# First unit of the first MoE as two half units of 128 tokens

## The chip, the cores and the metric

The kernel runs on one core of a Trainium2 chip. It is one program whose instructions stand in one queue per engine: TensorE (PE in the rows, its weight loads PEld), VectorE (DVE), ScalarE (ACT), GpSimd (POOL), and SyncE (SP), which issues the DMAs. The metric is the device time of one execution in microseconds (us); a kernel's time is the median of its runs.

## The reference

Attention with a bias that depends on the relative position, then two MoE layers on all 2304 tokens. Every output has to be close to the 32-bit reference, so the kernel splits operands into two 16-bit parts (high and low) and multiplies high by high, high by low and low by high.

```python
scores = scale * np.matmul(q, k.transpose(0, 1, 3, 2))       # 4 batches, 8 heads, 576 x 576
bias = np.maximum(x @ w1 + b1, 0.0) @ w2                     # x: from the relative position
attn = softmax(scores + bias)
x = np.matmul(attn, v)                                       # -> 2304 tokens x 512
g = x @ w_gate                                               # first MoE: 512 -> 1536 -> 512
x = (silu(g) * (x @ w_val)) @ w_out
h = np.maximum(x @ w_in, 0.0)                                # second MoE: 512 -> 2048 -> 512
out = h * h @ w_out2
```

## The kernel before

**Attention** goes over the queries in tiles: tile 0 has queries 0 to 127 of all batches and heads, then come tiles 1, 2, 3 and a merged one with the last 64 queries. A tile of 128 queries has 32 items, each one batch and one head, batch by batch; I number them from 1, so batch 0 is items 1 to 8, batch 1 items 9 to 16, and item 33 is the first of tile 1. An item is: scores on PE (4 matmuls, L813), bias and minimum on DVE (L822), the exponential on ACT (L827), five transposes on PE (L851, L853), a copy out of PSUM on ACT (L854), and the product with V on PE (L865, `av`). Before the items of a tile, and beside those of the tile ahead, the tile's bias is made (L644 on PE, masks L605 on DVE).

During tile 0 three more things go on. The keys are prepared in eight groups of four heads (`prep_k`): split into parts (L197 on POOL, L191 on DVE), turned by PE in three steps (L706) and copied out by ACT (L708); K group 4 serves items 17 to 20, group 6 items 25 to 28. The **weights stream** (`w_stream`) loads the three matrices of the first MoE, decodes them on DVE (L262, L265, L267), measures them (L324, L361, L328), and splits them (L191, L197, L201, L220). Gate and value come in three column groups, then `w_out` in 12 blocks of rows. The blocks of `w_out` from the eighth on overwrite the raw keys, so they wait for K group 7; the whole of `w_out` must be measured (its sum over partitions goes through PE at L139 and DVE at L141) before its 12 splits (L201 on ACT, L191 on DVE) can begin. The split of one block overwrites what the block after it reads, so the 12 go one after the other.

**The first MoE** works in units of 256 tokens (`moe1`). Unit 0 is batches 0 and 1 of tile 0, unit 1 batches 2 and 3 of it, and so on. When the attention of a unit's tokens is done, `finish_unit` takes their largest norm (a transpose on PE, a reduction on DVE), makes a scale of it on one partition (several DVE instructions on 1x1) and spreads it over the partitions with a matmul (L169), copies it (L908, L909), makes the two 16-bit parts of each 128 tokens in `xh` (L921 on ACT, L922 on DVE; one buffer), and turns them with a DMA into `xT` (L925). Then come 12 blocks of 128 hidden columns, 24 matmuls each on 256 columns (L459), gate and value side by side in one PSUM bank; tanh on ACT (L467), two products on DVE (L468, L470), which free the bank, and the split of the result into `z` (L444 on ACT, L220 on POOL). At the end 72 matmuls on 512 columns multiply `z` by `w_out` (L482), 36 for each half of the unit.

**PSUM** of this stage: `mm` has two banks, for the blocks of the unit, the accumulator of the product with `w_out`, and sums of the weights stream. `ma` is a single bank, for the turns of the keys and queries and for `finish_unit`; its users take turns in the order in which the program was recorded.

**What sets the order.** The instructions are recorded by two generators, attention with the weights stream (`a`) and the MoE units (`m`), each with a position in its own cost units. `m` takes a step when `a` has passed a base plus a table's value (`LEAD`) at `m`'s position. The base is `a`'s position when the first unit of attention is done. Tokens gate steps: `("unit", m)` waits for the attention of unit m, `("w", 3)`, ahead of the product with `w_out`, for the end of the weights stream, `("f", 2)` in that stream, after the second column group, for two blocks of the MoE. What was recorded is then put in order on each engine by the scheduler of the framework; within an engine the queue runs in that order.

## Time and profile before

| | |
|---|---|
| median of 3 runs | 1244.9 us (1240.95 to 1245.37) |
| the profiled execution, its own time | 1241.07 us |
| its span, first to last instruction | 1238.9 us |
| PE busy | 1089.9 us, 88% of the span |
| DVE busy | 778.1 us, 63% |
| ACT busy | 678.0 us, 55% |
| POOL busy | 651.8 us, 53% |
| TensorE clock granted, mean | 0.961 |

Busy shares are means over stages with different limits. Tile 0 of the attention runs to about 215 us, the bias of tile 1 is made from 235 us, tile 1's first item starts at 271 us, and attention ends near 705 us; the rest is the end of the first MoE and the second MoE. Rows of a timeline give start and duration, engine, line, operation, tiles and shape, and in brackets how long the engine had been idle and what ended that. Durations of matmuls overlap, so their cost is read from one start to the next.

### The profile page before, as it was taken

How to read it: one execution, taken by the hardware profiler on the slowest of the kernel's cores; microseconds unless marked ns; L12 is line 12 of the kernel's file. 1: busy time of each engine (PE TensorE's matmuls, PEld its weight loads, DVE VectorE, ACT ScalarE, POOL GpSimd, SP SyncE). 2: the span in 40 equal slices, each digit the busy share in tenths (PEclk: the TensorE clock that was granted, in tenths of full speed). 3: DMA queues.
4: the chain of work that ended last, by engine and by line, in shares of the span. 5: the costliest groups of instructions: out<-in, count | busy, mean ns of one | idle time of the engine just before them, and what ended most of it. 6: DMA issues, size and time to landing. Idle time of an engine off the chain costs nothing.

```text
span 1238.9 us, 27332 instructions
## 1 busy us (share of the span) xinstructions
PE 1089.9 (88%) x10550; PEld 812.1 (66%) x10550; DVE 778.1 (63%) x1864; ACT 678.0 (55%) x1370; POOL 651.8 (53%) x835
## 2 busy tenths in 40 slices
PE   2577899998678889999997999979789999999998
PEld 2466788686467568686774767556348476584787
DVE  5988957887677667656665745895573442624423
ACT  3567767557566566566663543366462643616433
POOL 2433213269768687878784452237791532705423
PEclk9789799999979999999999999989999999999999
DMA  9957543219999998997989995660010010010100
GB/s 222 263 136 206 179 132 87 50 58 198 222 218 204 227 212 165 231 186 162 191 161 257 248 220 142 206 188 1 17 34 19 18 43 27 20 33 17 27 27 17
DMA packets 278078, 163.20 MB, mean 132 GB/s; under 512 B 233276, under 2 KB 246588, under 8 KB 277948
## 3 DMA queue, kind: packets, MB, share of 16 engines
q1 hardware_dynamic: 277948, 161.46, 55.0%
q8 instruction: 82, 1.34, 0.5%
q14 instruction: 48, 0.39, 0.1%
HBM read 92.13 MB, written 19.48 MB: 90 GB/s over the span
## 4 chain that ended last, share of the span: by engine, by line
PE 45%; DMA 14%; POOL 10%; DVE 8%; issue 5%; ACT 4%; SPq 2%; POOLq 0%; ACTq 0%; DVEq 0%
PE mm L1377 12%; PE mm L459 11%; PE mm L1409 10%; DMA pT<-pt 3%; PE mm L482 3%; POOL pt L220 3%; POOL x L1189 2%; PE ma L1409 2%; PE av L875 2%; PE qk L813 2%; DMA w2s<-in_moe_w_out_dram 2%; DMA qT<-qs 2%; DMA scrap<-in_moe_w_in_dram 1%; DMA kp<-kT_d 1%; DMA xT<-xh 1%
## 5 line engine op out<-in xcount | busy, mean ns | idle before, releaser
L459 PE MATMUL mm<-xT,wr 128*128 128x256 f16 x2400 | 288.7, 276 | 14.9 <-DVE th L470 7.3
L459 PEld LDWEIGHTS <-wr 128*128 128x128 f16 x2592 | 251.6, 99 | 53.2 <-issue 19.3
L1189 POOL TENSOR_TENSOR x<-x 128x256 f32<-128x256 f32 (+1 forms) x160 | 142.7, 903 | 178.1 <-ACT x L1386 171.7
L220 POOL TENSOR_TENSOR pt<-s,pt 128x512 f16<-128x512 f32 x224 | 172.1, 791 | 31.5 <-ACT pt L837 26.7
L220 POOL TENSOR_TENSOR z<-th,z 128x256 f16<-128x256 f32 x108 | 79.8, 740 | 129.5 <-ACT z L444 124.7
L482 PE MATMUL mm<-wr,z 128*128 128x512 f16 x612 | 142.3, 379 | 1.6 <-DVE sc L829 1.3
L822 DVE CUSTOM_DVE_ANT_0 s<-qk,room 128x576 f32<-128x576 f32 x144 | 107.7, 748 | 39.9 <-PE qk L813 22.6
L1409 PEld LDWEIGHTS <-wr 128*128 128x128 f16 x1134 | 110.6, 98 | 22.7 <-DVE wr L1189 4.3
L830 ACT ACTIVATE s<-s,sc 128x576 f32<-128x576 f32 x112 | 85.6, 772 | 56.6 <-DVE sc L829 47.1
L1189 DVE TENSOR_TENSOR wr<-x,wr 128x768 f16<-128x768 f32 (+3 forms) x60 | 75.4, 1268 | 64.5 <-ACT wr L1196 63.3
L1377 PE MATMUL mm<-wr,w2r 128*128 128x512 f16 (+1 forms) x480 | 102.2, 364 | 5.0 <-ACT x L1382 5.0
L482 PEld LDWEIGHTS <-z 128*128 128x128 f16 x648 | 60.0, 98 | 66.4 <-issue 2.8
L605 DVE TENSOR_TENSOR scrap<-scrap,room 128x1024 f16<-128x1024 f16 (+1 forms) x108 | 87.3, 822 | 22.4 <-PE ma L644 19.8
L1377 PE MATMUL mm<-wr,room 128*128 128x512 f16 (+1 forms) x480 | 100.1, 358 | 0.0
L621 POOL TENSOR_TENSOR scrap<-scrap 128x256 f32<-128x256 f32 (+1 forms) x90 | 63.2, 702 | 65.9 <-ACT scrap L620 58.2
L875 PE MATMUL av<-vp,pT 128*128 128x65 f16 (+3 forms) x1792 | 70.4, 196 | 28.3 <-DMA pT<-pt 24.3
L875 PEld LDWEIGHTS <-pT 128*128 128x128 f16 (+1 forms) x1792 | 61.7, 102 | 43.2 <-DMA pT<-pt 32.7
L1377 PEld LDWEIGHTS <-w2r 128*128 128x128 f16 x480 | 47.6, 99 | 52.7 <-issue 8.6
L644 PEld LDWEIGHTS <-scrap 128*128 128x128 f16 x1440 | 59.6, 104 | 27.4 <-issue 11.9
L1377 PEld LDWEIGHTS <-room 128*128 128x128 f16 x480 | 46.9, 98 | 45.6
L1428 ACT ACTIVATE ob<-ob,fac 128x256 f32<-128x256 f32 x36 | 17.8, 506 | 105.5 <-DVE ob L1427 105.5
L444 ACT CAST z<-th 128x256 f16<-128x256 f32 x108 | 42.8, 399 | 59.0 <-DVE th L470 57.8
(289 smaller groups left out, 2157.2 us busy)
## 6 DMA issues: line engine op xcount, KB each, us to landing
kp<-kT_d SPq DMA_DIRECT2D x64, 288.0 KB, 3.5
vp<-v_d SPq DMA_DIRECT2D x48, 325.0 KB, 3.5
w2s<-in_moe_w_out_dram SPq DMA_DIRECT2D x16, 512.0 KB, 4.0
wr<-in_moe_w_gate_dram SPq DMA_DIRECT2D x24, 256.0 KB, 5.2
wst<-in_moe_w_out_dram SPq DMA_DIRECT2D x12, 512.0 KB, 4.0
wr<-in_moe_w_val_dram SPq DMA_DIRECT2D x24, 256.0 KB, 4.2
v_d<-vp SPq DMA_DIRECT2D x16, 325.0 KB, 3.1
y_d<-yh SPq DMA_DIRECT2D x18, 256.0 KB, 3.5
```

The lines of the kernel that those rows point to most:

```text
L220: nc.gpsimd.tensor_tensor(out=out_, in0=x, in1=hi, op=ALU.subtract)
L459: nc.tensor.matmul(pg[:, 256 * gi:256 * gi + 256], wr.parts(key, f // 4, cc, wl, P * (f % 4), P), mov(xl, cc), start=k == 0, stop=k == 11)
L482: nc.tensor.matmul(po, zall[:, f, zl, P * t:P * t + P], wr.parts("o", 0, f, wl), start=k == 0, stop=k == 3 * NF1 - 1)
L605: nc.vector.tensor_tensor(out=m[:, :, ni * e:ni * e + ni], in0=block(kb, i0, ni), in1=th, op=ALU.is_gt)
L621: nc.gpsimd.tensor_tensor(out=tmp[r], in0=tmp[r], in1=xb, op=ALU.mult)
L644: nc.tensor.matmul(pv[:, :, :, c:c + 4], m[:, a, :], bd[:, l], start=l == 0, stop=l == 1)
L822: nc.vector.tensor_tensor_reduce(out=s.rearrange("p (a j) -> p a j", a=2), in0=pq[:, :, 0:288], in1=bias[:, n].rearrange("p (a j) -> p a j ...
L830: nc.scalar.activation(s, s, AF.Exp, bias=nm, scale=-1.0)
L875: nc.tensor.matmul(av[r, slot, 0:cn], pT[:, 5 * l + c, r], vs[e][c][:, c0:c0 + cn], start=m == 0, stop=m == 13)
L1189: (nc.gpsimd if how else nc.vector).tensor_tensor(out=out_, in0=a, in1=b, op=op)
L1377: nc.tensor.matmul(ph[:, :n], w2r.parts("w", g // 4, cc, wl, P * (g % 4), P), yt[:, 4 * yl + cc, :], start=m == 0, stop=m == 11)
L1409: nc.tensor.matmul(po, HS[f][:, o:o + P], st["C7"][f][wl][:, b:b + 256], start=f == 0 and k == 0, stop=f == 7 and k == 2)
```

## The change

Unit 0 alone is computed as two half units. `finish_unit` is called after batch 0 and again after batch 1, each time for 128 tokens, and both write their half of one `xT`. `moe1` runs twice, first for the tokens of batch 0, then for those of batch 1, with the same instructions on 128 columns in place of 256. The product with `w_out` has as many instructions as before, 36 for each half, and the weights stream's gate for it stands: the first half's product and all of the second half are recorded after the end of the weights stream. The base is now `a`'s position at the end of batch 0, 11.2 cost units earlier; `LEAD` has 11.2 more at its points from 39 on, so that unit 1 and all units after it are recorded at the same places beside the attention as before.

```diff
-LEAD = [0, 39, 78, 117, 260, 400], [0, 85.669, 132.183, 165.544, 287.094, 406.094]
+LEAD = [0, 20, 39, 78, 117, 260, 400], [0, 48.0, 96.87, 143.383, 176.744, 298.294, 417.294]
+HALVED = (0,)
...
-    def moe1(m):
-
-        yield ("unit", m)
-        xt, sx = xT.pop(m), ux.pop(m)
+    def moe1(m, half=None):
+
+        yield ("unit", m if half != 0 else m - 0.5)
+        n = 256 if half is None else P
+        b0 = P if half else 0
+        xt, sx = xT[m, half], ux[m, half]
...
-                            pg[:, 256 * gi:256 * gi + 256], wr.parts(key, f // 4, cc, wl, P * (f % 4), P),
+                            pg[:, n * gi:n * gi + n], wr.parts(key, f // 4, cc, wl, P * (f % 4), P),
...
-            yield 2.6
+            yield 2.6 * n / 256
...
         yield ("w", 3)
-        for t in range(2):
+        for t in range(2) if half is None else (half,):
...
-    def finish_unit(u, xs_, nrm):
-
-        m1 = scr([P, 1], tag="fm")
-        nc.vector.tensor_reduce(out=m1, in_=nrm, axis=AX, op=ALU.max)
+    def finish_unit(u, xs_, nrm, half=None):
+
+        m1 = nrm
+        if half is None:
+            m1 = scr([P, 1], tag="fm")
+            nc.vector.tensor_reduce(out=m1, in_=nrm, axis=AX, op=ALU.max)
...
-        t = (mw2[0] if more else mw).tile([P, 2, 4, 256], F16, tag="xT", name="xT")
+        t = xT[u, 0] if half else (mw2[0] if more else mw).tile([P, 2, 4, 256], F16, tag="xT", name="xT")
...
-                if i == (3 if merged else 1):
+                u = state["u"]
+                if u in HALVED:
+                    yield ("fin", u)
+                    finish_unit(u, state["xs"], state["nrm"][:, 0:1], b % 2)
+                    done[0] = u - 0.5 if b % 2 == 0 else u
+                    state.update(u=u + b % 2, xs=[], nrm=None)
+                elif i == (3 if merged else 1):
...
-        if done[0] >= 0 and w_done[0] >= 0 and base is None:
+        if done[0] > -1 and w_done[0] >= 0 and base is None:
```

In the changed program the lines stand 1 to 14 further down (L706 is L711, L822 is L827, L921 is L928, L459 is L463, L482 is L487). Counted in the order of PE: before, the first matmul of unit 0 stands after the scores of item 24, 192 of its 288 stand ahead of the last items' products with V, and 96 of them and 41 of the 72 matmuls with `w_out` stand between the last product with V and the first matmul of tile 1's bias. Now there are 576 short ones. The first stands after the scores of item 16, 48 stand ahead of those of item 17, all 288 of the first half ahead of those of item 25, and none between those of items 25 and 32. The 288 of the second half and 66 of the 72 matmuls with `w_out` stand between the end of tile 0 and the first matmul of the bias. Of unit 1, 144 matmuls (six blocks) stood between that bias matmul and the scores of item 33, now 192 (eight blocks). From the scores of item 82 on, PE's order is the same row by row; the other engines' orders rejoin near the same place.

On PE, before, the first turn of K group 4 (the last row here) stands behind item 8's product with V, after the scores of item 9:

```order
L848 MATMUL tr<-qT,ident_h 128x512
L851 MATMUL tr<-ident,s 128x128 x4
L853 MATMUL tr<-ident,s 128x128
L865 MATMUL av<-wr,pT 128x64 x5
L706 LDWEIGHTS room_114
L706 MATMUL ma<-ident_h,room_114 128x128
```

On PE in the changed program the same turn (L711) stands behind the spread of the first half unit's scale in `ma` (the second L170), after the scores of item 16:

```order
L853 MATMUL tr<-qT,ident_h 128x512
L856 MATMUL tr<-ident,s 128x128 x4
L858 MATMUL tr<-ident,s 128x128
L870 MATMUL av<-room_114,pT 128x64 x10
L170 MATMUL mm<-sc,ones_r 128x2
L170 MATMUL ma<-sc,ones_r 128x2
L711 LDWEIGHTS room_114
L711 MATMUL ma<-ident_h,room_114 128x128
```

What moved is the turn: the half unit's two uses of the single bank now come ahead of it, and all three turns of the group stand together behind them.

On ACT, before, the two halves of unit 0's `xh` (L921) stand among the items, with the exponential of a later item behind the second:

```order
L361 ACTIVATE wst,keep_2097<-wr,keep_2091 128x512
L854 COPY pT<-tr 128x640
L827 ACTIVATE s,sc<-s,sc 128x576
L921 ACTIVATE xh<-room_114,ux 128x512
L854 COPY pT<-tr 128x640
L921 ACTIVATE xh<-room_114,ux 128x512
L827 ACTIVATE s,sc<-s,sc 128x576
L708 COPY kva<-ma 128x4x256
```

On ACT in the changed program the first half's `xh` (L928) stands alone, with the turned keys of group 4 (L713) and the first short tanh (L471) behind it; the second half's `xh` comes 53 rows later:

```order
L832 ACTIVATE s,sc<-s,sc 128x576
L362 ACTIVATE wst,keep_1873<-wr,keep_1865 128x512 x2
L928 ACTIVATE xh<-room_114,ux 128x512
L713 COPY kva<-ma 128x4x256 x2
L713 COPY kva<-ma 128x4x64
L362 ACTIVATE wst,keep_1873<-wr,keep_1865 128x512 x2
L471 ACTIVATE th<-mm,ux 128x128
```

What moved is that no second `xh` follows the first, and that work on `w_out` (L362) and the keys stand there instead.

On DVE, before, the measure of `w_out` (L364, then the copy of its sum, L141) stands among the products of unit 0's blocks, all 32 items' scores being past:

```order
L265 SCALAR_TENSOR_TENSOR wr<-wst,wr 128x512
L191 SCALAR_TENSOR_TENSOR wr<-wr,keep_2045 128x512
L470 SCALAR_TENSOR_TENSOR th<-th,mm 128x256
L267 SCALAR_TENSOR_TENSOR wr<-wst,wr 128x512
L468 SCALAR_TENSOR_TENSOR th<-th,mm 128x256
L191 SCALAR_TENSOR_TENSOR wr<-wr,keep_2045 128x512
L470 SCALAR_TENSOR_TENSOR th<-th,mm 128x256
L364 TENSOR_REDUCE sc<-keep_2097 128x1
```

On DVE in the changed program the same measure (L365, L142) stands among the last items (L827, the pair of rows that takes an item's scores), before those of item 32:

```order
L827 ISA s,sc<-qk,room_115 128x576
L827 ISA sc 128x1
L263 TENSOR_SCALAR wr<-wst 128x512
L756 COPY qs<-qs 128x4x64
L266 SCALAR_TENSOR_TENSOR wr<-wst,wr 128x512
L268 SCALAR_TENSOR_TENSOR wr<-wst,wr 128x512
L827 ISA s,sc<-qk,room_115 128x576
L827 ISA sc 128x1
L365 TENSOR_REDUCE sc<-keep_1873 128x1
L900 TENSOR_TENSOR room_114<-av,sc 128x256
L827 ISA s,sc<-qk,room_115 128x576
L827 ISA sc 128x1
```

What moved is the attention against the weights stream: in each stretch from item 17 on, the stream is further ahead of the items than it was.

## Rows read from the trace of the kernel before

**Rows 1.** Stretches of 20 us: busy us (instructions) of PE, PEld, DVE, ACT, POOL; clock, DMA share, GB/s.

```profile
120.00:140.00 20.00, 15.13 (x131) 13.39 (x131) 20.00 (x45) 15.42 (x31) 7.77 (x6) 0.91 0.68 211
140.00:160.00 20.00, 17.34 (x90) 15.11 (x90) 13.34 (x39) 10.75 (x25) 3.17 (x2) 0.59 0.56 169
160.00:180.00 20.00, 18.31 (x192) 16.70 (x192) 11.04 (x25) 16.42 (x31) 3.62 (x3) 0.99 0.28 78
180.00:200.00 20.00, 17.05 (x160) 15.16 (x160) 15.57 (x54) 18.62 (x42) 5.99 (x7) 1.00 0.52 151
300.00:320.00 20.00, 18.52 (x197) 11.33 (x197) 14.21 (x36) 14.99 (x34) 19.57 (x28) 1.00 1.05 221
```

**Rows 2.** Timeline of PE, items 24 and 25 and unit 0's first block.

```profile
160.74 0.65 PE L813 MATMUL qk<-room,qT 128*128 128x288 f16 x4
...
164.77 2.79 PE L459 MATMUL mm<-xT,wr 128*128 128x256 f16 x24
...
172.57 0.65 PE L813 MATMUL qk<-kva,qT 128*128 128x288 f16 x4
```

**Rows 3.** Timeline of ACT, the two halves of unit 0's xh.

```profile
153.51 0.71 ACT L921 ACTIVATE xh<-room,ux 128x512 f16<-128x512 f32 x1
...
160.07 0.72 ACT L921 ACTIVATE xh<-room,ux 128x512 f16<-128x512 f32 x1 [5.12 <-DMA xT<-xh]
```

**Rows 4.** Timeline of PE from tile 0's end to item 33.

```profile
176.43 0.61 PE L706 MATMUL ma<-ident_h,room 128*128 128x128 f16 x8
176.87 0.65 PE L813 MATMUL qk<-kva,qT 128*128 128x288 f16 x4
...
197.20 0.65 PE L813 MATMUL qk<-room,qT 128*128 128x288 f16 x4
...
230.35 5.14 PE L482 MATMUL mm<-wr,z 128*128 128x512 f16 x23
235.33 0.57 PE L644 MATMUL qk<-bd,scrap 128*128 128x64 f16 x14
...
256.67 2.78 PE L459 MATMUL mm<-xT,wr 128*128 128x256 f16 x24
259.29 1.10 PE L644 MATMUL qk<-bd,scrap 128*128 128x64 f16 x32
...
270.64 0.65 PE L813 MATMUL qk<-kp,qT 128*128 128x288 f16 x4
```

**Rows 5.** Timeline of ACT and DVE: what frees one block's bank.

```profile
167.60 0.48 ACT L467 ACTIVATE th<-mm,ux 128x256 f32<-128x256 f32 x1 [0.74 <-PE mm L459]
...
168.11 0.42 DVE L468 SCALAR_TENSOR_TENSOR th<-th,mm 128x256 f32<-128x256 f32 x1 [1.94 <-ACT th L467]
...
168.57 0.42 DVE L470 SCALAR_TENSOR_TENSOR th<-th,mm 128x256 f32<-128x256 f32 x1
```

**Rows 6.** DVE's instructions of 112 to 147 us by form: count, busy us, mean ns.

```profile
L191 DVE SCALAR_TENSOR_TENSOR wr<-wr,keep 128x512 f16<-128x512 f32 x6 | 4.5, 742 | 0.7 <-POOL wr L197 0.6
...
L191 DVE SCALAR_TENSOR_TENSOR room<-wr,room 128x1280 f16<-128x1280 f32 x2 | 3.0, 1476 | 0.0
L267 DVE SCALAR_TENSOR_TENSOR wr<-wst,wr 128x512 int32<-128x512 int32 x4 | 2.6, 674 | 0.0
...
L166 DVE TENSOR_SCALAR sc<-sc 1x1 f32<-1x1 f32 x2 | 0.3, 133 | 0.0
```

**Rows 7.** Timeline of PE, K group 4's first turn and item 17's scores.

```profile
99.79 0.61 PE L706 MATMUL ma<-ident_h,room 128*128 128x128 f16 x8
...
130.64 0.65 PE L813 MATMUL qk<-kva,qT 128*128 128x288 f16 x4
```

**Rows 8.** Timeline of DVE, w_out's sum and its first and last split.

```profile
213.13 0.15 DVE L141 COPY sc<-mm 1x1 f32<-1x1 f32 x1
...
216.62 0.75 DVE L191 SCALAR_TENSOR_TENSOR wr<-wr,keep 128x512 f16<-128x512 f32 x1 [0.59 <-ACT wr L201]
...
237.03 0.74 DVE L191 SCALAR_TENSOR_TENSOR wr<-wr,keep 128x512 f16<-128x512 f32 x1
```

More of the change, by code (lines that the diff above doesn't have):

```diff
@@ L437, in mov @@
             if m < 8:
-                return xt[:, l, cc, :]
+                return xt[:, l, cc, b0:b0 + n]
             pair = xt[:, l, 2 * (cc // 2):2 * (cc // 2) + 2, :].rearrange("p c t -> p (c t)")
@@ L443, in finish @@
             with tc.high_priority():
-                nc.scalar.copy(zall[:, f, 0, :], th)
-                rest_of(zall[:, f, 1, :], th, zall[:, f, 0, :])
+                hi, lo = [zall[:, f, l, b0:b0 + n] for l in range(2)]
+                nc.scalar.copy(hi, th)
+                rest_of(lo, th, hi)
         last = None
@@ L464, in moe1 @@
                     finish(f - 1, last)
-            last = mw.tile([P, 256], F32, tag="th", name="th", bufs=3)
+            last = mw.tile([P, 256], F32, tag="th", name="th", bufs=3)[:, 0:n]
             with tc.high_priority():
-                nc.scalar.activation(last, pg[:, 0:256], AF.Tanh, scale=cg)
+                nc.scalar.activation(last, pg[:, 0:n], AF.Tanh, scale=cg)
                 nc.vector.scalar_tensor_tensor(
-                    out=last, in0=last, scalar=1.0, in1=pg[:, 0:256], op0=ALU.add, op1=ALU.mult)
+                    out=last, in0=last, scalar=1.0, in1=pg[:, 0:n], op0=ALU.add, op1=ALU.mult)
                 nc.vector.scalar_tensor_tensor(
-                    out=last, in0=last, scalar=CZ, in1=pg[:, 256:512], op0=ALU.mult, op1=ALU.mult)
+                    out=last, in0=last, scalar=CZ, in1=pg[:, n:2 * n], op0=ALU.mult, op1=ALU.mult)
             f_done[0] += 1
-            yield 2.6
+            yield 2.6 * n / 256
         finish(NF1 - 1, last)
-        gv_done[0] = m
+        if half != 0:
+            gv_done[0] = m
         yield ("w", 3)
-        for t in range(2):
+        for t in range(2) if half is None else (half,):
             po = mx()
@@ L909, in finish_unit @@
         nc.vector.tensor_copy(sx[:, 1:2], pb[:, 0:1])
-        ux[u] = sx
+        ux[u, half] = sx
         w = 256 if u == 8 else 512
         more = u >= 2 and u % 3 == 2
-        t = (mw2[0] if more else mw).tile([P, 2, 4, 256], F16, tag="xT", name="xT")
+        t = xT[u, 0] if half else (mw2[0] if more else mw).tile([P, 2, 4, 256], F16, tag="xT", name="xT")
         tv = t.rearrange("p l (c d) t -> p l c (d t)", d=512 // w)
-        for i, xx in enumerate(xs_):
+        for i, xx in enumerate(xs_, half or 0):
             k = i * w // 512
@@ L927, in finish_unit @@
                 in_=xh.rearrange("p l e -> p (l e)"))
-        xT[u] = t
+        xT[u, half] = t
     done, w_done, gv_done, f_done, av_done = [-1], [-1], [-1], [0], [0]
@@ L1284, in m_all @@
         for m in range(9):
-            yield from moe1(m)
+            for h in (0, 1) if m in HALVED else (None,):
+                yield from moe1(m, h)
     sa, sm = a_all(), named(m_all(), "m")
```

## The prediction, made before the changed kernel had run

> **What bounds the kernel now.** I first cut the trace into stretches of 20 us [rows 1]. No engine bounds the end of tile 0's attention for long: DVE is busy throughout 120 to 140 us (decoding and splitting weights between the items), 140 to 160 us has every engine partly idle and a granted clock of 0.59 (much of it at the lower level, 1.2 GHz), and from 160 us PE leads with 18.31 and 17.05 of 20 us. In tile 1 POOL (19.57 of 20) and the DMA engines (share 1.05) are full, so there the attention no longer waits for the MoE. What the change can win or lose must therefore show in when item 33, the first of tile 1, starts, now at 270.64 us [rows 4]. Everything behind it follows its predecessors, and from item 82 on PE's order is the same. So the forecast is the shift of item 33, less what tile 1 gives back.
>
> Next I looked for waits around unit 0 in the timelines. Item 25's scores come 11.8 us after item 24's [rows 2], where the seven gaps from item 25 to item 32 take 172.57 to 197.20, 24.6 us, 3.5 us each [rows 2, 4]. In that gap ACT waits 5.12 us for the single `xh` buffer to be read by the first transposing DMA [rows 3], with item exponentials queued behind it. Last, after tile 0 PE does unit 0's remaining blocks and the product with `w_out`, and the bias comes behind them at 235.33 us [rows 4]; that product is held by the 12 splits of `w_out`, which end at 237.8 us, 24.6 us after its sum at 213.13 [rows 8].
>
> **The arithmetic.** PE: 24 matmuls on 256 columns take 2.62 us from start to start, 109 ns each [rows 4], so the unit costs 288 x 109 = 31.4 us. A turn, 128 columns with weights of its own, takes 0.44 us for 8, 55 ns [rows 4]; 576 x 55 = 31.7 us. The doubled weight loads hide, and PE pays nothing. DVE and ACT get 24 instructions more each, POOL 12. A product on 128 columns is not in the trace; it lies between a 1x1 instruction, 0.13 us [rows 6], and the 256-column one, 0.42 us [rows 5]. Two against one then cost between -0.16 and +0.42 us; I take 0.28 us for one, the middle, so +0.14, and 24 x 0.14 = 3.4 us of DVE spread over 100 us in which it has gaps. On the path I count it at nothing while items hide it; uncovered it is 3.4 us (bounds -3.8 to 10). The second `finish_unit` is some ten tiny DVE instructions at 0.13, 1.3 us, and no extra DMA: two transposes as before, now a batch apart.
>
> The Trainium skill bears on these extra instructions, page Perfetto Trace Analysis, section Optimizing Scalar/DVE Operations: each carries a fixed access cost, about 125 ns for DVE on PSUM, and larger operations pay if the engine is saturated. That speaks against the change; by it the 24 products would be 3.0 us (an estimate), beside the 3.4 above, and no row yet has a 128-column one.
>
> **Item 17 moves back.** The new order puts both uses of the `ma` bank by the first half's `finish_unit` ahead of K group 4's turns, which item 17 needs. The first turn ran at 99.79 us, item 17's scores at 130.64 [rows 7]. In DVE's new queue eight more decoding steps (0.67), four splits of weights (0.74), one of keys (1.48), the half's own low part (about 0.74) and four short products (0.28) stand between items 16 and 17 [rows 6]: 5.4 + 3.0 + 1.5 + 0.7 + 1.1 = 11.7 us on an engine that is full just then [rows 1]. Item 17: 130.6 + 11.7 = 142.3. The time isn't lost: the weights stream is ahead by it.
>
> **Items 17 to 25.** All 240 remaining matmuls of the first half stand here, 13.1 us. The gaps of items 25 to 32 held two blocks, 48 x 109 ns = 5.2 us, so a gap without MoE is (24.6 - 5.2)/7 = 2.8 us. Eight of them and the matmuls: 22.2 + 13.1 = 35.3 us if PE is the limit, 8 x 3.5 = 28 if half the matmuls hide. The second half's `finish_unit` again stands ahead of K group 6's turns; of today's long gap, 11.8 - 2.8 - 5.1 = 3.9 us would recur without the wait for `xh`. I take 38, nearer to the first, since PE is already at 86 to 92% there. Item 25: 142 + 38 = 180 (170 to 186), now 172.6.
>
> **The sum of `w_out`.** With its last decoding waiting for K group 7, the sum now comes after item 31. Six gaps of 2.8 are 16.8, and two loads that have to land add about 2: 180 + 19 = 199 (189 to 207), now 213.1. This is the gain of the change, 14 us.
>
> **The bias of tile 1.** Today it starts 22.2 us after that sum (235.33 - 213.13). In the new order the 288 matmuls of the second half (15.8 us) and 66 of the product stand in between; 23 of those take 230.35 to 235.33, 217 ns each [rows 4], so 14.3 us. By PE alone, with the last items and the first split (216.62 + 0.75 is 4.2 us after the sum [rows 8]), about 5 + 15.8 + 14.3 = 35 us. By the splits, the first half's 36 products end no sooner than 24.6 us after the sum; then come 30 more (6.5 us) and some 130 short matmuls (7.1 us): 38 us. I take 40, for both are met only if nothing slips. Bias at 199 + 40 = 239, 4 us later than now: the gain is spent, since the product and the whole second half had to wait for the same sum.
>
> **To item 33.** Now 270.64 - 235.33 = 35.3 us, with 31 products (6.7 us) and six blocks of unit 1 (15.7). Afterwards 6 products (1.3) and eight blocks (20.9), so 35.3 - 5.4 + 5.2 = 35 if idle stays, 31 if it closes. I take 33: item 33 at 272, +1.4 us. Two blocks of unit 1 are then already done, and tile 1, full on POOL, may return up to 1.5 us. The sum is about zero: 1241 us for an execution like the profiled one (1241.07, span 1238.9), and 1245 us against the median of 1244.9, which lies 3.8 us above it.
>
> **Rivals.** (1) **Faster: the attention hides the first half.** If items 17 to 25 keep today's mixed pace, 28 us and the 3.9 of the finish, item 25 comes at 174 and the sum at 193; with 38 and 33 behind it item 33 is at 264, -6.6 us, about 1237 with tile 1's part. For it: ACT's wait of 5.12 us goes, and DVE has gaps of 9 of 20 us after 160 [rows 1]. Against it: PE is the fullest engine there.
>
> (2) **Slower: the banks in the burst.** With 256 columns a block keeps PE for 2.62 us, and its bank is free 0.48 + 0.42 + 0.42 and small gaps, 1.4 us, after its last matmul [rows 5]; with two banks that hides. A short block lasts 1.3 us. While the product holds one of the two `mm` banks, each block waits for the bank of the one before it; if tanh and products take nearly as long as now, or find a split ahead of them (0.74), the wait is 1.4 + 0.7 - 1.3 = 0.8 us a block, 12 x 0.8 = 10 us in the burst, where nothing else can fill it: 1255. It decides from the point where freeing a bank takes longer than the 1.3 us of other matmuls put beside it. The order puts five or six products there, 1.1 to 1.3 us, and a short chain would be about 0.34 + 2 x 0.28 = 0.9.
>
> (3) **Slower: the clock.** From 140 to 160 us PE was granted 0.59, after 20 us in which it was busy 15.13 [rows 1]. With item 17 moved back, PE does less between 128 and 142 us. If the first half's 240 matmuls run at 1.2 GHz, they cost 13.1 us more, two thirds of it on the path since PE leads: +8, 1253. The skill's page TensorE: Matmul & The Clock Gate, section What's actually happening, has the array throttled by default and activity lifting that; by this rule the dense first half would soon raise the clock, which speaks for a smaller price.
>
> That the change does not do what it says is ruled out for the first half by the order (its blocks stand beside items 17 to 24); that the second half gains nothing is in the sum.
>
> **How the numbers follow.** Forecast, no change: 0.48. Rival 1: 0.27. Rival 2: 0.13. Rival 3: 0.12. One measurement of this kernel can tell about 0.5%, 6 us, from no change. Rival 1 lies at that edge and takes most of faster, with a part of the forecast's lower tail; so faster 0.26, same 0.49, slower 0.25. The predicted time is the likeliest case's, 1245. Its own terms (item 25 from 170 to 186, the bias 35 to 42 behind the sum, 31 to 35 to item 33) reach some 8 us to either side when a few of them err together; with the rivals at 1237, 1253 and 1255, leaving out their far tails, the range is 1235 to 1256.
>
> **What would show it.** In the new trace: item 17's scores near 142 us, item 25's near 180, `w_out`'s sum near 199 and thus before item 32, no wait of ACT for `xh` in tile 0, the first bias matmul some 40 us behind the sum, item 33 near 272, and the shift there kept to the end. Item 33 before 265 would be rival 1; gaps before the short matmuls of the burst that DVE ends are rival 2; a granted clock near 0.5 from 142 to 165 us is rival 3. The forecast is wrong in kind if the shift at item 33 isn't the shift at the end.

## The result: 1.1% slower

The changed kernel takes 1259.6 us (median of 6 runs, 1256.6 to 1265.2) against 1245.2 us (6 runs, 1241.0 to 1251.0); the ratio is 1.0111, 95% interval 1.0079 to 1.0144. Four further runs of it in a later series gave 1.0137 (1.0088 to 1.0185). The forecast was no change, 1245 us in a range up to 1256: wrong in kind, and the time lies outside the range.

The profiled execution took 1264.80 us (span 1262.7), 5 us above the median; the profiled one of the kernel before lay 4 us below its own. So of the 23.7 us between the two traces some 14 stand for the kernels.

The stretches of the changed kernel that answer to [rows 1], and the one behind them:

```profile
120.00:140.00 20.00, 13.06 (x107) 11.39 (x107) 18.88 (x52) 9.94 (x21) 8.97 (x7) 0.78 0.54 152
140.00:160.00 20.00, 16.64 (x221) 15.57 (x219) 15.55 (x42) 19.09 (x45) 5.91 (x7) 0.97 0.63 201
160.00:180.00 20.00, 19.13 (x240) 18.11 (x239) 14.91 (x52) 13.98 (x32) 8.68 (x11) 1.00 0.30 77
180.00:200.00 20.00, 14.92 (x170) 13.30 (x168) 15.47 (x39) 17.04 (x38) 4.41 (x5) 0.98 0.51 175
200.00:220.00 20.00, 20.00 (x130) 17.50 (x130) 9.74 (x36) 11.11 (x22) 0.00 (x0) 0.67 0.23 47
```

PE is fuller from 160 to 180 us, as meant, but emptier from 180 to 200 (14.92 against 17.05 us), and then full at a granted clock of 0.67, much of it at 1.2 GHz. The marks on PE's timeline that answer to [rows 2, 4, 7] (first use of `ma` by the first half's `finish_unit`, its second use, first turn of K group 4, item 17, item 25, item 32, first bias matmul, item 33):

```profile
106.36 0.27 PE L132 MATMUL ma<-ident,sc 128*1 128x128 f32 x1
...
130.40 0.36 PE L170 MATMUL ma<-sc,ones_r 1*128 1x2 f32 x2
131.99 1.01 PE L711 MATMUL ma<-ident_h,room 128*128 128x128 f16 x8 [1.23 <-DVE ux L916]
...
144.08 0.65 PE L818 MATMUL qk<-kva,qT 128*128 128x288 f16 x4
...
185.32 0.65 PE L818 MATMUL qk<-kva,qT 128*128 128x288 f16 x4
...
210.76 1.17 PE L818 MATMUL qk<-room,qT 128*128 128x288 f16 x4
...
252.79 0.60 PE L649 MATMUL qk<-bd,scrap 128*128 128x64 f16 x15
...
285.73 0.65 PE L818 MATMUL qk<-kp,qT 128*128 128x288 f16 x4
```

And DVE's that answer to [rows 8], `w_out`'s sum and its first and last split:

```profile
208.17 0.14 DVE L142 COPY sc<-mm 1x1 f32<-1x1 f32 x1
...
214.93 0.75 DVE L192 SCALAR_TENSOR_TENSOR wr<-wr,keep 128x512 f16<-128x512 f32 x1 [0.82 <-ACT wr L202]
...
232.42 0.75 DVE L192 SCALAR_TENSOR_TENSOR wr<-wr,keep 128x512 f16<-128x512 f32 x1 [0.27 <-ACT wr L202]
```

The sum comes 5.0 us earlier than before, not 14; item 33 15.1 us later, not 1.4.

### The profile page after: what moved, and what is told of

It reads as the page before. It is cut to its first block, busy times and chain, and to the rows that moved or that the text cites. A ratio compares the mean times of both kernels' runs of the same rounds, so it can differ in the third digit from the quotient of the medians.

```text
span 1262.7 us, 28025 instructions
## 1 busy us (share of the span) xinstructions
PE 1105.3 (88%) x10841; PEld 824.6 (65%) x10841; DVE 780.5 (62%) x1899; ACT 683.9 (54%) x1394; POOL 658.5 (52%) x847
## 4 chain that ended last, share of the span: by engine, by line
PE 44%; DMA 19%; DVE 12%; POOL 11%; issue 6%; ACT 5%; SPq 1%; POOLq 0%; ACTq 0%; DVEq 0%
PE mm L1391 12%; PE mm L1423 10%; PE mm L463 8%; PE mm L487 5%; DMA pT<-pt 5%; POOL pt L221 3%; DMA qT<-qs 3%; POOL x L1202 2%; PE ma L1423 2%; PE qk L818 2%; DMA wr<-in_v_dram 2%; PE av L880 2%; DMA wr<-in_k_dram 2%; POOL z L221 1%; DVE s L827 1%
## 5 line engine op out<-in xcount | busy, mean ns | idle before, releaser
L463 PE MATMUL mm<-xT,wr 128*128 128x256 f16 (+1 forms) x2688 | 295.3, 265 | 18.4 <-DVE th L474 7.4
L463 PEld LDWEIGHTS <-wr 128*128 128x128 f16 x2880 | 260.8, 100 | 62.3 <-issue 24.6
L221 POOL TENSOR_TENSOR z<-th,z 128x256 f16<-128x256 f32 (+1 forms) x120 | 86.1, 720 | 165.0 <-ACT z L448 159.1
L487 PE MATMUL mm<-wr,z 128*128 128x512 f16 x612 | 146.7, 383 | 0.7 <-DVE th L474 0.4
L827 DVE CUSTOM_DVE_ANT_0 s<-qk,room 128x576 f32<-128x576 f32 x144 | 108.0, 750 | 50.3 <-PE qk L818 36.3
L1423 PEld LDWEIGHTS <-wr 128*128 128x128 f16 x1134 | 110.7, 98 | 20.5 <-DVE wr L1202 3.0
L487 PEld LDWEIGHTS <-z 128*128 128x128 f16 x648 | 60.6, 99 | 65.2 <-issue 4.9
L610 DVE TENSOR_TENSOR scrap<-scrap,room 128x1024 f16<-128x1024 f16 (+1 forms) x108 | 88.9, 838 | 18.7 <-PE ma L649 13.8
L448 ACT CAST z<-th 128x256 f16<-128x256 f32 (+1 forms) x120 | 44.9, 377 | 61.0 <-DVE th L474 60.6
```

The lines of the kernel that those rows point to most:

```text
L221: nc.gpsimd.tensor_tensor(out=out_, in0=x, in1=hi, op=ALU.subtract)
L463: nc.tensor.matmul(pg[:, n * gi:n * gi + n], wr.parts(key, f // 4, cc, wl, P * (f % 4), P), mov(xl, cc), start=k == 0, stop=k == 11)
L487: nc.tensor.matmul(po, zall[:, f, zl, P * t:P * t + P], wr.parts("o", 0, f, wl), start=k == 0, stop=k == 3 * NF1 - 1)
L610: nc.vector.tensor_tensor(out=m[:, :, ni * e:ni * e + ni], in0=block(kb, i0, ni), in1=th, op=ALU.is_gt)
L827: nc.vector.tensor_tensor_reduce(out=s.rearrange("p (a j) -> p a j", a=2), in0=pq[:, :, 0:288], in1=bias[:, n].rearrange("p (a j) -> p a j ...
L1423: nc.tensor.matmul(po, HS[f][:, o:o + P], st["C7"][f][wl][:, b:b + 256], start=f == 0 and k == 0, stop=f == 7 and k == 2)
```

## Experiments, first part: where is the loss?

Three theories stood at first. A: the first half's `finish_unit` holds `ma` (106.4 to 131.7 us), item 17 is late for it, and that lives on. B: the second half has to wait for `w_out`'s sum and makes a burst behind tile 0. C: short blocks cost time by themselves. D was formed on the first four runs: what counts is how much MoE work PE still has between items 32 and 33.

**e1_bank.** Only the first half's two turns move to the `mm` banks:

```diff
-        r = expo(pmax(m1, ma), half=True)
-        pb = spread(r, (2.0 ** 49, 2.0 ** -50), ma)
+        bank = mx if half == 0 else ma
+        r = expo(pmax(m1, bank), half=True)
+        pb = spread(r, (2.0 ** 49, 2.0 ** -50), bank)
```

> The changed kernel with one edit: the first half unit's finish_unit takes its two PSUM turns from the mm banks and not from the single ma bank, so K group 4's turns no longer stand behind it. Theory A (the hold of ma, 106.4 to 131.7 us in the changed kernel, delays item 17 by 13.4 us and that delay lives on to the end): item 17's scores return to 130 to 133 us, item 33's come at 272 to 276, time 1246 to 1250. Theory B (the first half has to share PE and DVE with the items, and the second half waits for w_out's sum anyway): item 17 returns to 130 to 133 too, but item 25 is at 180 or later and item 33 stays at 282 to 287, time 1256 to 1262.

Measured: 1268.5 us, ratio 1.0174 (1.0122 to 1.0226). Its timeline of PE, item 17, the second half's two uses of `ma`, item 25:

```profile
128.67 0.65 PE L818 MATMUL qk<-kva,qT 128*128 128x288 f16 x4
...
140.25 0.42 PE L132 MATMUL ma<-ident,sc 128*1 128x128 f32 x1
...
179.71 0.58 PE L170 MATMUL ma<-sc,ones_r 1*128 1x2 f32 x2
...
190.09 0.65 PE L818 MATMUL qk<-kva,qT 128*128 128x288 f16 x4
```

Item 17 is on time, but the second half now holds `ma` for 39 us and item 25 comes 5 us later still. Items 32 (210.2) and 33 (285.6) stand where they stood, as theory B had it; the time lies above the forecasts of both. Theory A is not refuted by this, since the hold moved; but the gain at item 17 was worth nothing.

**e3_short.** The halves stay, the early start goes: both `finish_unit` calls at the end of batch 1, base and table as before.

```diff
-                    finish_unit(u, state["xs"], state["nrm"][:, 0:1], b % 2)
-                    done[0] = u - 0.5 if b % 2 == 0 else u
+                    if b % 2 == 0:
+                        state["pf"] = (state["xs"], state["nrm"][:, 0:1])
+                    else:
+                        finish_unit(u, *state["pf"], 0)
+                        finish_unit(u, state["xs"], state["nrm"][:, 0:1], 1)
+                        done[0] = u
```

> The changed kernel with both half units finished together at the end of batch 1, and with base and table of the kernel before: the short blocks and their gates without the early start. Theory A (hold of ma): item 17 near 131 and item 33 within 3 us of the kernel before (271 to 274), time 1244 to 1248. Theory B (the second half, gated by w_out's sum, leaves a burst behind tile 0 and two more blocks of unit 1 ahead of item 33): sum to item 33 still takes some 75 us, item 33 at 284 to 290, time 1256 to 1262. Theory C (short blocks cost time by themselves, through banks and DVE): as B, with idle time of PE ahead of short blocks that DVE ends.

Measured: 1270.3 us, 1.0190 (1.0151 to 1.0230). Items 17 (129.7), 25 (171.2) and 32 (198.6) are where they were in the kernel before, and item 33 is at 287.7, 17 us late. All but 1.4 us of that loss arises behind item 32. With item 17 on time the loss is larger than the changed kernel's, so theory A can't be the whole explanation.

**e4_gvfirst and e5_bank_gvfirst.** Both products with `w_out` move behind the blocks of both halves; the second has e1's edit too.

```diff
-        yield ("w", 3)
-        for t in range(2) if half is None else (half,):
+        if half == 0:
+            return
+        yield ("w", 3)
+        for t in range(2):
+            iu = ux[m, None if half is None else t][:, 5:6]
```

> The changed kernel with both products with w_out behind the blocks of both halves, so that the second half's blocks are no longer gated by w_out's sum and can stand among items 25 to 32. Theory A: item 17 stays at 144, item 33 at 283 to 286, time 1257 to 1261. Theory B: no stretch at 1.2 GHz between items 28 and 32 (199 to 213 us in the changed kernel), sum to bias under 38 us instead of 45, item 33 at 275 to 279, time 1249 to 1254.

> Both edits, mm banks for the first finish_unit and products behind both halves. If the two losses add (A and B each in part): item 17 at 130 to 133, item 33 at 264 to 270, time 1238 to 1244, ahead of both kernels. If A alone holds: 1246 to 1250. If PE's work to item 33 sets the time whatever the order: item 33 at 274 to 280, time 1248 to 1254.

Measured: 1259.5 us, 1.0100 (1.0061 to 1.0140), and 1269.1 us, 1.0184 (1.0143 to 1.0224). In e4 the stretch at 1.2 GHz behind item 28 is mostly gone and the bias starts at 243.5, but item 32 comes at 217.2; item 33 at 281.4 (between the two theories) won 4 us, the time nothing. e5 missed by far: item 25 at 197.5, item 33 at 289.7.

**e6_short_gvfirst** is e3 with e4's edit: short blocks, and nothing else of the change.

> Only the short blocks: both half units are finished together at the end of batch 1, base and table are those of the kernel before, and both products with w_out stand behind the blocks of both halves, as in the kernel before. The order of PE has 10 of unit 0's 12 blocks and none of the products ahead of the bias, and 3 blocks fewer of unit 1 ahead of item 33 than before. Theory C (short blocks cost time by themselves): time 1254 to 1262, with idle time of PE that DVE or ACT ends ahead of short blocks. Theory D (what counts is how much MoE work PE still has between items 32 and 33: that stretch was work left plus 21 to 24 us in the kernel before, the changed one and three of the four kernels run so far): 10.65 blocks of 2.62 us, products 15.6 us and 22, so item 33 at 199 + 65 = 264 us, and since 3 blocks (7.9 us) are left for later, time 1240 to 1248.

Measured: 1250.9 us, 1.0035 (1.0010 to 1.0061); item 33 at 269.5, bias at 226.2. Theory C is out as the explanation: short blocks cost at most 0.6%. (The time lies between the forecasts of C and D.) And it differs from e3 in nothing but the place of the first half's product, and so in the second half's blocks no longer waiting for the weights stream; together this is worth 19 us. Its products, on PE's timeline, stand beside the bias:

```profile
238.81 5.56 PE L490 MATMUL mm<-wr,z 128*128 128x512 f16 x25 [0.39 <-DVE th L474]
...
245.14 5.13 PE L490 MATMUL mm<-wr,z 128*128 128x512 f16 x23
...
251.04 5.13 PE L490 MATMUL mm<-wr,z 128*128 128x512 f16 x23
```

**e7_bank2, e8_bank2_gvfirst, e9_before_bank**: both halves' turns on the `mm` banks; the same with e4's edit; and the kernel before with unit 0's turns there.

> The changed kernel with both half units' finish_unit on the mm banks (the run before had the first one only, and the delay moved from item 17 to item 25). Theory A in its new form (each finish_unit that holds ma delays the next K group's turns by 10 to 20 us, the delay lives on): item 17 near 130, item 25 at 165 to 175, item 32 at 194 to 200, time 1246 to 1251. Theory D: item 32 at 194 to 200 with 3.5 blocks of unit 0 done, work left 8.5 + 7 blocks and the products, 40.6 + 15.6 + 22 = 78 us, item 33 at 272 to 278, time 1248 to 1254. If only the gate of the second half counts, as in the run with the late finish: 1264 to 1272.

> Both finish_units on the mm banks and both products behind the blocks of both halves. Theory D: item 32 at 194 to 200 with 3.5 blocks done, 10.5 blocks, products and 22, 27.5 + 15.6 + 22 = 65 us, item 33 at 260 to 265, four blocks of unit 1 (10.5 us) left for later, time 1238 to 1248. Theory A alone: as the run with both finish_units on mm, 1246 to 1251. Theory C: above 1254.

> The kernel before with unit 0's finish_unit on the mm banks, no halves. Its hold of ma, 144.4 to 152.3 us, goes. Theory A: the 11.8 us gap ahead of item 25 shrinks to 4 to 8, item 25 at 164 to 168 instead of 172.6, item 32 at 188 to 194, time 1237 to 1243. Theory D: item 32 at 190 to 195 with 3 blocks done, 14 blocks, products and 22, 74 us, item 33 at 264 to 269, one block left for later, time 1240 to 1246.

Measured: 1275.4 us, 1.0236 (1.0203 to 1.0269); 1266.9 us, 1.0163 (1.0134 to 1.0193); 1243.0 us, 0.9983 (0.9965 to 1.0000). Without the hold of `ma` item 32 comes at 191.9, 192.6 and 188.8, 5 to 8 us before the old 197.2, and item 33 at 294.2, 284.9 and 267.7. e7 is the clearest: 19 us ahead of the changed kernel at item 32, 8.5 us behind it at item 33. Its time ends theory A in its newer form too (each hold of `ma` delays what follows; 1246 to 1251 expected); e8 was as slow as only theory C had it, which e6 rules out. Theory D fits e9 (264 to 269) but put e7 at 272 to 278 and e8 at 260 to 265, so as a rule for item 33 it falls as well.

## Experiments, second part: the scratch tile

What the slow kernels share stands on ACT. The timeline of ACT in the changed kernel: the square of the first half's product (L498), the values' norm (L675), the squares of batches 2 and 3 (L970), and unit 1's `xh` (L928):

```profile
234.39 0.60 ACT L498 ACTIVATE junk<-mm 128x512 bf16<-128x512 f32 x1
...
235.10 1.06 ACT L675 ACTIVATE junk<-kva 128x1024 bf16<-128x1024 f32 x1
...
237.84 0.62 ACT L970 ACTIVATE junk<-room 128x512 bf16<-128x512 f32 x1
...
240.74 0.62 ACT L970 ACTIVATE junk<-room 128x512 bf16<-128x512 f32 x1
...
246.03 0.72 ACT L928 ACTIVATE xh<-room,ux 128x512 f16<-128x512 f32 x1
```

Batch 3's last product with V ended near 219 us, and its square, which opens unit 1's `finish_unit`, comes some 22 us later. In the kernel before, ACT's timeline has the two in the other order:

```profile
214.85 0.63 ACT L963 ACTIVATE junk<-room 128x512 bf16<-128x512 f32 x1 [0.80 <-DVE sc L166]
...
243.34 0.59 ACT L493 ACTIVATE junk<-mm 128x512 bf16<-128x512 f32 x1
```

All these squares want only their sum; the squared values go to one scratch tile, `junk1`. In this program writers of one tile keep the order in which they were recorded. Before, unit 0's product is recorded behind all of tile 0. In the change the first half's product follows its blocks at once when the weights stream ends, at 144.7 of `a`'s cost units, when 22 of the 32 items are recorded to their end. So batch 2's and 3's squares wait for `w_out`'s sum, 12 splits, 36 products and that square. Unit 1's `xh` then frees the room (L928, L929 read it) that tile 1's bias is built in, with the angles from which the masks are made (L597 to L610): in all kernels run the first bias matmul comes 2.6 to 6.9 us after unit 1's first `xh` on DVE, and item 33 33 to 46 us after the bias. This is theory J. It fits the order of ACT in every run: where the product is recorded first (the changed kernel, e1, e3, e7), batch 3's square stands 6.3 to 6.4 us behind the product's and 22 to 33 us behind the last product of its own batch; in the others, within 2.1 us of that.

The end of this chain in the changed kernel, on POOL (the room is cleared as soon as `xh` has been read), DVE (the first two masks) and PE (the work just ahead of the first bias matmul at 252.79):

```profile
247.60 0.10 POOL L597 MEMSET room<- 128x1 f32 x1 [1.17 <-DVE xh L929]
```

```profile
248.04 1.53 DVE L610 TENSOR_TENSOR scrap<-scrap,room 128x1024 f16<-128x1024 f16 x2
```

```profile
250.40 2.55 PE L487 MATMUL mm<-wr,z 128*128 128x512 f16 x11
```

So the masks are ready 3.2 us before the bias, and PE goes from the product to the bias without a pause. From the sum to the bias PE idled only 3.3 of 44.6 us. Two limits thus lie close together here: the chain, which allows no bias before about 249 us, and PE's queue, which has 288 short matmuls and 66 products ahead of it. The second seems to follow from the first: when the chain is cut, PE's order changes with it (below).

**e10_junk, e11_bank2_junk, e12_short_junk**: the square of the product writes to `yh`, which is overwritten next, in the changed kernel, in e7 and in e3.

```diff
-        nc.scalar.activation(junk_tile()[:, 0:512], po, AF.Square, accum_out=ss)
+        yh = mw.tile([P, 2, DM], F16, tag="yh", name="yh", bufs=1)
+        nc.scalar.activation(yh[:, 0, :].bitcast(BF16), po, AF.Square, accum_out=ss)
...
-        yh = mw.tile([P, 2, DM], F16, tag="yh", name="yh", bufs=1)
```

> The changed kernel with one edit: the square of the product with w_out in out_y writes its unused result into yh and no longer into the scratch tile junk1. Theory J: in the changed kernel the squares of batches 2 and 3 of tile 0, which open unit 1's finish_unit, and the norms of the values write junk1 too and are recorded behind that square of the first half's product, so they wait for w_out's sum, 12 splits and 36 products (ACT: the square at 234.4 us, batch 2's and 3's at 237.8 and 240.7, though the last product with V was at 218.9); unit 1's xh frees the room that the bias masks need, so bias and item 33 wait as well. With the edit: squares within 3 us of their batches' last products, unit 1's first xh at 222 to 230, bias at 226 to 234, item 33 at 266 to 274 instead of 285.7, time 1240 to 1250. Theory D (PE's work sets it): item 33 earlier by as much, but the 8 blocks of unit 1 that the order now leaves behind item 33 come back in tile 1, 1256 to 1262. If neither, item 33 at 284 to 287.

> The kernel with both finish_units on the mm banks (1275 us) with the same edit of the scratch tile. Theory J: its items 17 to 32 were 13 to 19 us earlier than in the changed kernel and that was lost behind the same square; now item 32 stays at 190 to 195, bias at 226 to 234, item 33 at 262 to 270, time 1238 to 1248. Theory D: 1256 to 1270.

> The kernel with the late start and the gated second half (1270 us) with the same edit of the scratch tile. Theory J: it was on time at item 32 (198.6 us) and lost 17 us behind the square; now bias at 222 to 230, item 33 at 262 to 270, time 1244 to 1252, near the kernel with the products behind both halves (1251). Theory D: 1262 to 1270.

e10 on ACT (batch 3's square, unit 1's `xh`) and on PE (first bias matmul, item 33):

```profile
221.32 0.61 ACT L970 ACTIVATE junk<-room 128x512 bf16<-128x512 f32 x1
...
227.48 0.71 ACT L928 ACTIVATE xh<-room,ux 128x512 f16<-128x512 f32 x1
```

```profile
231.41 1.17 PE L649 MATMUL qk<-bd,scrap 128*128 128x64 f16 x32
...
269.87 0.65 PE L818 MATMUL qk<-kp,qT 128*128 128x288 f16 x4
```

e12 on PE, the same two marks:

```profile
220.33 0.71 PE L649 MATMUL qk<-bd,scrap 128*128 128x64 f16 x13
...
255.56 0.66 PE L818 MATMUL qk<-kp,qT 128*128 128x288 f16 x4
```

This one edit brings the bias 21.4 us forward and item 33 15.9 (e10), 34.3 and 32.1 us (e12). It changes PE's order too: ahead of the bias stand 96 short matmuls and 28 products in e10 in place of 288 and 66, and from item 32 on 103 and 4 in e12 in place of e3's 408 and 66. How much of the gain is the wait itself and how much the new order can't be told apart in these runs; both come with the one link. e12 takes 1248.3 us, 1.0029 (1.0001 to 1.0057), where e3 had 1.0190: all but 0.3% of the loss of e3 is gone. The second half still waits for `w_out`'s sum in e12, so this also ends theory B, which e3 and e6 had left open, as the explanation of e3's loss. e11 takes 1264.5 us, 1.0144 (1.0085 to 1.0203); item 33 moved from 294.2 to 275.9, and its other trouble, last products with V that end at 227 us behind a `spread` on the `mm` banks, stayed.

At the marks theory J was right in e10, and in e12 they came earlier still than it said. For the time of the whole kernel it was right in e12 (1244 to 1252 expected) and wrong in e10 and e11, which it put at 1240 to 1250 and 1238 to 1248; both came out where theory D had them (1256 to 1262, 1256 to 1270), whose reason was that work that is put off comes back. In the changed kernel itself less of it reaches the end: e10 takes 1257.0 us, 1.0093 (1.0062 to 1.0123), and the interval overlaps those of the changed kernel (1.0111 and 1.0137), so a gain in time isn't shown. The changed kernel's four runs beside it (r1, below) have a median 6.4 us higher, but reach from 1259.0 to 1266.0 us where e10's nine reach from 1251.5 to 1265.8. In the traces 15.9 us at item 33 are 11.5 at item 86 and 9.4 at the end. In the order of PE 20 blocks of unit 0 and 1 stood ahead of item 33 and now 12.25; the other 7.75, 20.3 us of PE, come back in tiles 1 and 2. e12 shows it most clearly: its item 33 stands 15.1 us ahead of the kernel before's, with 10 blocks and 36 products ahead of it in place of 18 and 72, and needs 993.3 us from there to the end in place of 968.3. So a gain at item 33 counts at the end only as far as the same work stands ahead of it.

## Experiments, third part: the early start

e10 and e12 ran on the same chip and differ in the early start alone, 8.7 us (their intervals do not overlap). e13 takes it apart, e10 with base and table of the kernel before; e18 and e19 ask for the value of the hold, r1 and r2 repeat both kernels.

**e13_finearly_junk**

> Early finish_unit of batch 0, but base and table of the kernel before, and the square of out_y in yh: between the run with the early start (1257 us) and the one with the late start (1248 us), both with that scratch edit. If the early finish_unit (its hold of ma ahead of K group 4's turns) is what the early start costs: item 17 at 142 to 145, time 1254 to 1260. If the early recording of the blocks is: 1246 to 1250, with item 17 near 131.

Measured: 1252.4 us, 1.0050 (1.0017 to 1.0083), between the two and not apart from either. The traces say more. Item 17 is late (142.5) as in e10 (143.2), so the early `finish_unit` does that; but item 32 comes at 203.3, 7.5 us before e10's, with the same six blocks done. The stretch from item 25 to item 32, of e10 and then of e13:

```profile
185.80:210.80 25.00, 19.77 (x144) 17.29 (x145) 17.09 (x44) 19.71 (x43) 1.65 (x3) 0.80 0.51 150
```

```profile
177.00:203.30 26.30, 22.23 (x260) 20.10 (x258) 19.66 (x58) 21.83 (x53) 7.00 (x9) 1.00 0.52 151
```

In e10, as in the changed kernel, all six blocks are spent ahead of item 25, so seven items take 25.0 us with no block beside them, at a mean clock of 0.80. In e13 they take 26.3 us with two and a half blocks (6.6 us of matmuls), at 1.00. That the blockless stretch costs e10 its time is so read from one trace of each and not shown by their times.

**e18_short_bank_gvf, e19_before_bank_lead**: e6 with both finishes on the `mm` banks; e9 with `LEAD`'s 85.669 as 78.0.

> Short blocks, late start, products behind both halves (1251 us) with both finish_units on the mm banks. If the hold of ma costs: item 25 at 160 to 166 instead of 174, item 33 at 262 to 267, time 1242 to 1248. If it is lost again behind tile 0: item 33 at 267 to 272, time 1248 to 1254.

> The kernel before with unit 0's finish_unit on the mm banks (ratio 0.998 in its run) and the table's second value 78.0 instead of 85.669, so that one more block of unit 0 and 19 products stand ahead of the bias. If deferred work was what took the gain back: item 33 at 266 to 270, time 1238 to 1243. If the bias comes later for it: item 33 at 270 to 274, time 1243 to 1248.

Measured: 1254.4 us, 1.0060 (1.0033 to 1.0087), item 33 at 271.9 though item 32 was at 191.8; 1249.8 us, 1.0018 (0.9994 to 1.0043), item 33 at 271.2. Both lie near the second case of their expectation. Time won ahead of item 32 is lost by item 33 once more; what holds the bias in these two I did not test. No kernel beats the one before clearly; e9 is the nearest (0.9983, up to 1.0000).

**r1_after_again, r2_before_again**

> The changed kernel itself, for a second profiled execution. If the shift at item 33 is the shift at the end: item 33 at 284 to 287 again, and between item 33 and the end 967 to 977 us (977 in the first profile, 968 in the kernel before). If something behind tile 0 costs 7 us more by itself, 975 to 979 again.

> The kernel before itself, a second profiled execution. If its first profile had a fortunate stretch behind item 33: item 33 at 269 to 272 and 971 to 977 us from there to the end instead of 968. If not: 966 to 970, and the changed kernel loses 9 us of its own behind item 33.

r1 took 1263.3 us (median): item 33 at 284.9, 979.0 us from there to the end (977.0 in the first profile). r2 took 1250.5 us, with item 33 at 280.0. Stretches from item 17 to 32, 32 to 33 and 33 to the end, of the kernel before's first execution and then of r2:

```profile
130.64:197.20 66.56, 56.96 (x483) 50.84 (x481) 46.77 (x133) 51.47 (x111) 14.96 (x13) 0.87 0.48 146
197.20:270.64 73.44, 69.61 (x765) 55.90 (x763) 58.28 (x148) 40.51 (x90) 31.80 (x39) 1.00 0.21 58
270.64:1238.90 968.26, 884.83 (x8477) 639.02 (x8476) 564.87 (x1335) 511.22 (x1030) 559.96 (x732) 0.98 0.56 127
```

```profile
132.50:203.50 71.00, 62.23 (x483) 55.93 (x482) 45.52 (x130) 51.80 (x110) 13.86 (x14) 0.79 0.45 137
203.50:280.00 76.50, 73.18 (x765) 58.30 (x764) 57.44 (x146) 39.98 (x89) 32.35 (x39) 0.95 0.20 56
280.00:1248.60 968.60, 887.02 (x8477) 639.84 (x8476) 566.98 (x1335) 511.12 (x1030) 560.96 (x732) 0.97 0.56 127
```

Two executions of one program differ by 9.4 us at item 33, with clocks of 0.79 and 0.95 in place of 0.87 and 1.00, and by 0.3 behind it. So the changed kernel's 977 to 979 us behind item 33 are its own, 8 to 11 more than the 968 to 969 of the kernel before; and its shift at item 33 against a middling execution of the kernel before is smaller than the 15.1 of the first pair (4.9 against r2). Of the 14.4 us between the medians some 4 to 6 are then left for all that stands ahead of item 33: an estimate from two traces of each kernel.

## Why the prediction was wrong, step by step

| step | predicted | measured |
|---|---|---|
| item 17 | 142 | 144.1 |
| item 17 to item 25 | 38 | 41.2 |
| item 25 to `w_out`'s sum | 19 | 22.9 |
| sum to the bias | 40 | 44.6 |
| bias to item 33 | 33 | 32.9 |
| item 33 | 272 | 285.7 |
| behind item 33 | up to 1.5 back | 8.7 more |

Two steps failed. The gain of 14 us at `w_out`'s sum did not come: the sum stood at 208.2 us (207.4 in r1) in place of 199, and 9.2 of the 13.7 us by which item 33 missed its 272 had arisen by then. And "everything behind it follows its predecessors", with up to 1.5 us returned, was wrong: 8 to 11 us were lost behind item 33. By the prediction's own last sign, a shift at item 33 (15.1) that isn't the shift at the end (23.7), it was wrong in kind. The second step is the surer one, since it is the same in both executions of either kernel; its cause stays open.

**Item 17 moves back** was right in mechanism and size: the first turn of K group 4 at 131.99 us stands behind the second use of `ma` at 130.40. "The time isn't lost" was wrong in size against the execution that it was worked out from: of 14 us by which the sum was to come earlier, 5.0 came. (In r2, the slower execution of the kernel before, the sum came at 223.0, so one pair does not fix the gain.)

**Items 17 to 25** held all 240 matmuls and the second finish, as said. Item 25 at 180 was 5.3 us too early, 2.1 from item 17 and 3.2 from here.

**The sum** failed on a point that was in my own text: no block stands between items 25 and 32. I priced their gaps at 2.8 us as a gain, at the full clock; they came out at 3.6 (25.4 us for seven). From 199.5 us to item 32 PE was busy throughout at 0.50, that is 1.2 GHz:

```profile
199.50:210.76 11.26, 11.26 (x56) 10.25 (x54) 5.02 (x20) 5.36 (x13) 0.00 (x0) 0.50 0.23 48
```

At full speed, if nothing else had held it, the same work would have taken 5.6 us less, and (25.4 - 5.6)/7 is 2.8 (an estimate; r1 has the same stretch, 198.5 to 209.9 us). So the price of a gap was about right, and the fall of the clock in this stretch is what it lacked; the 2 us for two loads, for which no row was given, came out at 1.9. Rival 3 had the clock fall from 142 to 165 us, where it was 0.97 and 1.00; it fell from about 131 to 142 and from 199 to 213 us, the second time after a stretch in which PE had been busy 14.92 of 20 us. The Trainium skill, page TensorE: Matmul & The Clock Gate, section What's actually happening, has the default throttled and activity release it. The trace agrees in part: the dense first half ran at 1.00 and the thin stretch behind it led to 0.50, but the lower level then lasted some 13 us with PE busy throughout.

**The bias** was right as a sum for the order that I had read: I took 40 us from PE's work (35) and the splits (38), and 44.6 came, with PE busy for 41.3 of them. What it had wrong is the reason. I wrote that the gain is spent because the product and the second half had to wait for the sum, and took it that the bias has to stand behind them. The chain that puts it there I did not have: sum, splits, first half's product, its square into `junk1`, the squares of tile 0's batches, unit 1's `finish_unit`, its `xh`, the room, the masks. e10 and e12 cut it at one link, and the bias came 21 and 34 us sooner, ahead of most of that work. It could have been read beforehand: both squares show `junk` as their output in ACT's timeline of the kernel before, and the change has the first of them recorded ahead of the others.

**Rival 2, the banks**, was small. DVE's and PE's groups by form from 200 to 256 us of the changed kernel:

```profile
L463 PE MATMUL mm<-xT,wr 128*128 128x128 f16 x288 | 18.8, 219 | 2.9 <-DVE th L474 1.6 <-DVE yh L506 1.3
...
L474 DVE SCALAR_TENSOR_TENSOR th<-th,mm 128x128 f32<-128x128 f32 x12 | 3.4, 285 | 0.3
L472 DVE SCALAR_TENSOR_TENSOR th<-th,mm 128x128 f32<-128x128 f32 x12 | 3.4, 284 | 2.8 <-ACT th L471 2.7
```

PE idled 2.9 us ahead of the second half's 288 matmuls, not 10, and the short product took 0.285 us where 0.28 was taken. Two of them cost 0.15 us more than one of 0.42, which is the part that does not shrink with the columns. The Trainium skill, page Perfetto Trace Analysis, section Optimizing Scalar/DVE Operations, gives about 0.125 us as the fixed part of such an access on PSUM; the 0.15 of the trace lies near it. With e6 (4.4 us by its ratio, for 3.4 uncovered), the costing of the short blocks was right.

**To item 33** was right to 0.1 us, and the returns behind it were wrong in sign. PE's order is the same from item 82 on, and most of the loss arises in the 250 us behind that item. From there to 519.8 us ahead of the end it is 249.4 us before (249.0 in r2) and 258.0 in the changed kernel (257.0 in r1):

```profile
469.70:719.10 249.40, 228.59 (x2784) 177.21 (x2781) 161.99 (x494) 147.89 (x319) 177.31 (x269) 0.99 0.94 202
```

```profile
484.90:742.90 258.00, 235.24 (x2817) 181.17 (x2815) 166.40 (x500) 150.61 (x324) 186.09 (x281) 0.97 0.95 201
```

The lower clock makes up 0.03 x 258 - 0.01 x 249, about 5 us of the 8.6, and since the clocks are given to two digits this may be 2.5 us off. From item 82 to the end PE also waited for `pT`, the turned exponentials that a DMA brings, 12.8 us in 14 waits where it had been 8.6 in 7 (10.3 in 13 in r1, 8.3 in 8 in r2), and POOL, which makes their low parts, had 522 instructions left at item 82 where it had been 514 or 515. That these are the cause no run tested; it stays open.

So, of the 14 us, by edits instead of by place: the halves as such cost about 4 us (e6, e12), and the early start another 8.7 (e10 against e12), perhaps in part by the blockless items 25 to 32. The scratch tile costs 20 us where the start is late (e3 against e12) and moves item 33 by 15.9 in the changed kernel; how much of that reaches its end, 2 to 6 us by the medians, is not settled.

## What to carry to other kernels

When work is recorded earlier, list every buffer that it writes and ask who else writes it later, scratch tiles for unwanted outputs included: one such tile put tile 0's squares behind a product for which nobody was waiting. Name the chain that releases the next stage (here a scale, a copy and a room), not only the work that stands ahead of it on the busiest engine. Work that is moved into an early gap leaves a later one empty; look at what then stands there. And a mark in the middle of a kernel stands for its end only if the same work lies behind it.

## What the runs showed of the hardware

Two executions of the kernel before, the same instructions in the same order, reached item 33 at 270.6 and 280.0 us, with mean granted clocks of 0.87 and 0.79 between items 17 and 32, and then needed 968.3 and 968.6 us to the end. A difference of less than some 10 us at a mark in that stretch, read from one trace each, is therefore no finding, and several of those above (item 17 to 25, the sum, item 33 of e4) are of that size. The 32 us at item 33 between e3 and e12, and the 20 us between their times, are.
